# The output projection of a fused attention and multiplicative FFN kernel, taken apart a second time: 49 small matrix products for 64, with streamed weight sums

## The chip, the core and the metric

The kernel runs on one NeuronCore of a Trainium2 chip. Its engines work side by side, each with an instruction queue of its own: TensorE (PE in the profile, with PEld for its weight loads), VectorE (DVE), ScalarE (ACT), GpSimd (POOL) and SyncE (SP), which here only issues DMAs. Time is the device time of one execution in microseconds (us), lower is better. A run of the kernel is compared by the median of several executions; one further execution is profiled, and every duration below comes from that one.

## What is computed

The attention is linear (no softmax): for each of 8 batches and 8 heads, with 576 tokens of 64 features, `kv = k^T v`, `out = q kv`, then an RMS norm over the 64 features with a gain. The result is laid out as 4608 tokens by 512 features and goes through

```
def _moe_ref(x, w1, w2, w3, w_out):
    a = x @ w1                 # 512 -> 1024
    b = x @ w2
    h = a * b @ w3             # 1024 -> 1024
    return (h @ w_out)         # 1024 -> 512, float32
```

All matrix products are done in float32. The weights arrive as 8-byte floats, and the kernel turns them into float32 itself.

## The kernel before, in words

**Fold.** `w3 @ w_out` is computed first, once: a 1024 by 512 matrix, `w3o_sb`, in 2 halves of 8 chunks. For each chunk, ACT and DVE convert raw words to float32 (`conversion`, L130), PE turns the chunk of w3 (`turn_w3`, L464), ACT copies it, and PE multiplies it with the chunk of w_out (`fold_chunk`, L477). Chunk numbers below count from 0, so the second chunk is chunk 1 (the "chunk 2" of the change's name). In this stage the order of DVE, ACT, SP and PE is written out by hand. `keep_warm` (L253) issues products of a constant matrix, whose results nobody reads.

**Groups.** The tokens are then worked on in 9 groups of 512: first 512 tokens of batches 0 to 6 (T = 0 to 6), then the 64 left-over tokens of all 8 batches together (T = 8), then batch 7 (T = 7). For each group:

- *Gates* (L613): four passes p = 0 to 3, each a two by two block product in 7 block products where plain multiplication has 8 (`winograd`, L489; the scheme is Winograd's form of Strassen's). It needs sums of blocks on both sides: `sum_w` and `combine_x`. Each pass has 28 matrix products of 128x128 by 128x256, and leaves `a * b` for 256 of the 1024 features in `ab`.
- *Projection* (L632): `ab @ w3o`, once more by 7 block products, of 8 matrix products each. Its sums are `sum_ab(p)` over `ab` (4 DVE operations per p) and `combine_w3o` over the weights (once, in group 0).

A matrix product in float32 is two instructions (MATMUL) in the trace, each with its own LDWEIGHTS. So 28 products are 56 MATMUL rows, and a whole projection of 56 products is 112.

The attention of the next batch is cut into 8 pieces (`steps`), which `between()` puts between the block products of the gates. `combine_x` for the next group is written ahead of the projection. PE's order is the written order; DVE, ACT and GpSimd run in an order that a scheduler fixed at build time, each engine strictly in its order. SP's DMA queue is in order too: a DMA whose wait is not over holds all behind it.

**Memory in the projection.** `allocate_projection` (L569) reuses the four conversion buffers (`raw`) for the sums over `ab`, the sums over `w3o` and the two output tiles. Results leave PSUM through `keep` (an ACT copy) and `done` (a DVE addition). There are 5 PSUM banks for all of this.

Lines L482 to L535 of the kernel before, which the prediction names by the profile's groups: L496 is the one line of all block products, L509 the ACT copy, L548 and L549 the DVE sums over `ab` and `w`, L538 the DVE sums over `x` and `w3o`, L618 and L619 the copy and the product of the last gate block (c21), L622 and L623 the same for the others.

Of the kernel before, what the change touches and what calls it, by code (L numbers as in the profile page):

```python
# [11 lines left out]
FP32 = mybir.dt.float32  # L12
# [8 lines left out]
def kernel(  # L21
# [32 lines left out]
    nc = tc.nc  # L54
# [58 lines left out]

    NF = KF // 2

    ab = [const.tile([P, 4, N], FP32, name=f"ab{p}") for p in range(NF)]

    w_sb = const.tile([P, KF, 2, NP, P], FP32, name="w_sb")
    w3o_sb = const.tile([P, KF, DM], FP32, name="w3o_sb")
# [10 lines left out]
    def conversion(n, dst, raw, cols=slice(0, 1024)):  # L130

        dst, raw = (t if len(t.shape) == 3 else t[:, cols] for t in (dst, raw))
        if raw.dtype == FP32:
            yield
            nc.vector.tensor_copy(out=dst, in_=raw)
            return
        words = raw.bitcast(U32).rearrange("p (n w) -> p n w", w=2)
        lo, hi = words[:, :, 0], words[:, :, 1]

        low = ab[NF - 2 + n % 2].rearrange("p i t -> p (i t)")[:, cols]  # L140
        low_bits = low.bitcast(U32)
        if len(dst.shape) == 3:
            wide = dict(c=dst.shape[1])
            lo, hi, low, low_bits = (
                t.rearrange("p (c n) -> p c n", **wide) for t in (lo, hi, low, low_bits)
            )
        dst_bits = dst.bitcast(U32)
        nc.scalar.activation(low, lo, AF.Copy, scale=2.0 ** -51, bias=2.0)  # L148
        nc.scalar.activation(dst, hi.bitcast(FP32), AF.Abs)
        yield  # L150
        nc.vector.scalar_tensor_tensor(  # L151
            out=low_bits, in0=hi, scalar=0x80000000, in1=low_bits,
            op0=ALU.bitwise_and, op1=ALU.bitwise_or,
        )
        nc.vector.tensor_scalar(
            out=dst, in0=dst, scalar1=LEAST, scalar2=MOST, op0=ALU.max, op1=ALU.min
        )
        nc.vector.tensor_scalar(
            out=dst_bits, in0=dst_bits, scalar1=3, scalar2=None, op0=ALU.logical_shift_left
        )  # L160
        nc.vector.tensor_tensor(out=dst_bits, in0=dst_bits, in1=low_bits, op=ALU.add)  # L161
# [12 lines left out]
    def raw_tile():  # L174
        return conv_pool.tile([P, 1024], w1.dtype, name="raw", bufs=RAW)
# [32 lines left out]
    def conversions(n):  # L208

        what, i = todo[n]  # L210
        if what == "w":
            return [conversion(n, w_sb[:, i].rearrange("p w c f -> p (w c f)"), raws[n])]
        if what == "b":
            return [conversion(n, chunks[:, 2 * i:2 * i + 2, 0, :], raws[n])]
        dst = chunks[:, i].rearrange("p w f -> p (w f)")
        cuts = [0, 1024] if i else [0, 256, 512, 1024]
        return [conversion(n, dst, raws[n], slice(a, b)) for a, b in zip(cuts, cuts[1:])]

    begun = []
# [40 lines left out]
    def attention(b):  # L260
# [74 lines left out]
        def product(h):  # L335

            o_ps = [bank(ps_at, "at") for _ in range(2)]
            for m in range(4):  # L340
                r, e = 2 * h + m // 2, m % 2
                for i in range(2):
                    n = 2 * m + i
                    for t in range(2):
                        tokens = slice(t * L, (t + 1) * L)
                        for l in range(2):
                            rows = slice(l * D, (l + 1) * D)
                            nc.tensor.matmul(  # L348
                                o_ps[l][tokens, n * D:(n + 1) * D],
                                lhsT=qT[r][rows, e, i, tokens],  # L350
                                rhs=kv_b[rows, e, r, :],
                                start=True,
                                stop=True,
                            )
            xn = st[h] = work.tile([P, 2, 2, 4, D], FP32, name="xn")
            return norm(o_ps, [xn[:, :, l].rearrange("p i m d -> p m i d") for l in range(2)])

        def product_left():
# [105 lines left out]
    def turn_w3(half, c):  # L464
        t_ps = bank(ps_at, "at").rearrange("p (m f) -> p m f", m=NH)
        for m in range(NH):
            src = chunks[:, c, 0, m * P:(m + 1) * P]
            nc.tensor.transpose(t_ps[:, m, :], src, ident)  # L468

        w3T[half, c] = ab[c % 4 // 2][:, c % 2 * 2:c % 2 * 2 + 2, :].rearrange(  # L470
            "p i (a f) -> p (i a) f", f=P
        )
        nc.scalar.copy(w3T[half, c], t_ps)
# [3 lines left out]
    def fold_chunk(half, c, ms):  # L477
        if c == 0 and 0 in ms:
            sums_ps[half] = [bank(ps_mm, "mm") for m in range(NH)]
        for m in ms:  # L480
# [4 lines left out]
            if c == KF - 1:  # L485
                nc.scalar.copy(w3o_sb[:, half * NH + m, :], sums_ps[half][m])


    def winograd(lhsT, rhs, chunks, done, between=lambda: None):  # L489

# [14 lines left out]
            return ps  # L505

        def keep(name, ps):
            t = late_pool.tile([P, 2, N], FP32, name=name[0] if name[0] == "u" else name)
            nc.scalar.copy(t, ps)  # L509
            return t  # L510

# [40 lines left out]
    def run(*step_lists):  # L552

        for steps in zip(*step_lists):
            for step in steps:
                step()
# [1 line left out]
    xb, wa, aa, ob = {}, {}, {}, {}  # L558
    xc = const.tile([P, 3, NP // 2, N], FP32, name="xc")
    free = {("w", 0): const.tile([P, 3, 2, NP // 2, P], FP32, name="ws0")}  # L560
    o_sbs = []

    def allocate():

# [3 lines left out]

    def allocate_projection():  # L569

        blocks = []
        for i in range(RAW):
            words = raw_tile().bitcast(FP32).rearrange("p (n t) -> p n t", t=N)
            if i + 1 < RAW:
                blocks += [words[:, n] for n in range(8)]
            else:
                o_sbs.extend(
                    words[:, 4 * n:4 * n + 4].rearrange("p (m j) t -> p m (j t)", m=2)
                    for n in range(2)
                )  # L580
        for p in range(NF):
            free["ab", p], free["w3o", p] = blocks[6 * p:6 * p + 3], blocks[6 * p + 3:6 * p + 6]

    def parts(t):
        return [t[:, i] for i in range(3)]
# [1 line left out]
    def combine_x(T):  # L587
        xb[T] = {f"b{i + 1}{j + 1}": xT[T][:, i, j] for i in range(2) for j in range(2)}
        return combine(xb[T], parts(xc))
# [7 lines left out]
        return sums(wa[p], parts(free["w", p]))  # L597

    def sum_ab(p):
        aa[p] = {name: ab[p][:, i, :] for i, name in enumerate(("a11", "a21", "a12", "a22"))}  # L600
        return sums(aa[p], free["ab", p])

    def combine_w3o(p):
# [4 lines left out]
        return combine(ob[p], free["w3o", p])  # L608


    AB_OF = {"c11": 0, "c12": 1, "c21": 2, "c22": 3}

    def gates(T, p, between):  # L613
        def done(name, one, two):
            dst = ab[p][:, AB_OF[name], :]
            if two is None:
                c = late_pool.tile([P, N], FP32, name="c21")
                nc.scalar.copy(c, one[:, 0, :])  # L618
                nc.vector.tensor_mul(dst, c, one[:, 1, :])  # L619
                return  # L620
            c = late_pool.tile([P, 2, N], FP32, name="c")
            nc.vector.tensor_add(c, one, two)  # L622
            nc.vector.tensor_mul(dst, c[:, 0, :], c[:, 1, :])  # L623

        winograd(
            lambda name, w, c: wa[p][name][:, w, c, :],
            lambda name, c: xb[T][name][:, c, :],
            NP // 2, done, between,
        )


    def project(T, between=lambda: None, last=False):  # L632
        def store(half):
            if T < B:
                rows = out[T * S:T * S + G, :].rearrange("(p j) f -> p j f", j=J)
# [6 lines left out]
                        out=out[b * S + G:(b + 1) * S, :], in_=o_sbs[half][l * L:(l + 1) * L, m, :]  # L642
                    )

        def done(name, one, two):
            half, j = int(name[1]) - 1, int(name[2]) - 1
            dst = o_sbs[half][:, :, j * N:(j + 1) * N]
            if last:

                rows = out[T * S:T * S + G, j * N:(j + 1) * N].rearrange("(p j) f -> p j f", j=J)  # L650
                parts = ((0, 1), (1, 2)) if two is None else ((0, 2),)
                for a, b in parts:
                    if two is None:
                        nc.scalar.copy(dst[:, a:b], one[:, a:b])
                    else:
                        nc.vector.tensor_add(dst, one, two)
                    queue = nc.scalar if a else nc.sync
                    queue.dma_start(out=rows[:, 2 * half + a:2 * half + b, :], in_=dst[:, a:b])
                return
            if two is None:  # L660
                nc.scalar.copy(dst, one)
            else:
                nc.vector.tensor_add(dst, one, two)  # L663
            if name in ("c11", "c21"):
                store(half)

        winograd(
            lambda name, m, p: aa[p][name][:, m * P:(m + 1) * P],
            lambda name, p: ob[p][name],
            NF, done, between,  # L670
        )


    ctx.enter_context(tc.manual_schedule(engines={mybir.EngineType.PE}))
# [4 lines left out]
    with tc.manual_schedule(  # L679
# [22 lines left out]
        for c in range(KF):  # L702
# [13 lines left out]
            fold_chunk(0, c, range(NH - 1))  # L716
            turn_w3(*((0, c + 1) if c + 1 < KF else (1, 0)))
            fold_chunk(0, c, [NH - 1])


        first = batch(0)
# [41 lines left out]
    for n, T in enumerate(groups):  # L763
# [19 lines left out]
        last = n + 1 == NG  # L783
        if T and not last:
            run(combine_x(groups[n + 1]))
        project(T, between if T == 0 else lambda: None, last)
        if T == 0:
            run(combine_x(1))


# [28 lines left out]
```

## Time and profile before

| What | us |
|---|---|
| median of 5 executions (lowest, highest) | 812.66 (811.55, 813.68) |
| the profiled execution's own time | 813.68 |
| its span, from the first to the last instruction | 811.9 |
| PE busy in it | 802.2 (99%) |
| DVE, ACT, POOL busy | 364.6, 264.8, 1.8 |
| projection of T = 1, first product to the next group's first product | 228.88 to 253.06 |
| data moved by DMA | 59.53 MB, mean 73 GB/s |

An engine's idle time matters only where PE waits for it. The granted TensorE clock was 0.998 of full speed over the span, so a stretch of PE rows shows how many instructions there were and little else, apart from the first 20 us. Times of rows are counted from the span's start.

### The profile page before, as it was taken

How to read it: one execution, taken by the hardware profiler on the slowest of the kernel's cores; microseconds unless marked ns; L12 is line 12 of the kernel's file. 1: busy time of each engine (PE TensorE's matmuls, PEld its weight loads, DVE VectorE, ACT ScalarE, POOL GpSimd, SP SyncE). 2: the span in 40 equal slices, each digit the busy share in tenths (PEclk: the TensorE clock that was granted, in tenths of full speed). 3: DMA queues.
4: the chain of work that ended last, by engine and by line, in shares of the span. 5: the costliest groups of instructions: out<-in, count | busy, mean ns of one | idle time of the engine just before them, and what ended most of it. 6: DMA issues, size and time to landing. Idle time of an engine off the chain costs nothing.

```text
span 811.9 us, 12622 instructions
## 1 busy us (share of the span) xinstructions
PE 802.2 (99%) x5335; PEld 677.8 (83%) x5335; DVE 364.6 (45%) x680; ACT 264.8 (33%) x501; POOL 1.8 (0%) x8
## 2 busy tenths in 40 slices
PE   7999999999999999999999999999999999999998
PEld 4455788888888888888888888888888888888887
DVE  6967997325431544154315441553145415422431
ACT  5677643233312432133214331332133212211220
POOL 0000000000000000000000000000000000000000
PEclk9999999999999999999999999999999999999999
DMA  9996551123102410231023101410100010002001
GB/s 314 300 328 182 185 144 40 53 78 92 52 1 79 104 53 1 78 92 53 0 78 105 52 1 54 116 53 1 55 24 1 1 52 1 1 0 52 1 0 52
DMA packets 60811, 59.53 MB, mean 73 GB/s; under 512 B 15316, under 2 KB 57300, under 8 KB 60756
## 3 DMA queue, kind: packets, MB, share of 16 engines
q1 hardware_dynamic: 60608, 58.60, 23.4%
q8 instruction: 42, 0.69, 0.4%
q10 hardware_dynamic: 148, 0.13, 0.0%
q14 instruction: 13, 0.11, 0.0%
HBM read 49.28 MB, written 9.44 MB: 72 GB/s over the span
## 4 chain that ended last, share of the span: by engine, by line
PE 98%; DMA 1%; DVE 0%; SPq 0%; ACT 0%; issue 0%; ACTq 0%
PE mm L496 81%; PE mm L481 7%; PE at L278 3%; PE at L348 2%; PE at L297 2%; PE at L381 2%; DMA raw<-in_moe_w_out_dram 1%; PE at L468 1%; PE at L366 0%; SPq L184 0%; PE at L390 0%; PE at L307 0%; DVE chunks L161 0%; DVE ab L151 0%; ACT ab L148 0%
## 5 line engine op out<-in xcount | busy, mean ns | idle before, releaser
L496 PE MATMUL mm<-xT,w_sb 128*128 128x256 f32 x768 | 176.2, 379 | 0.0
L496 PEld LDWEIGHTS mm<-xT,w_sb 128*128 128x128 f32 x768 | 145.9, 190 | 20.3 <-issue 0.5
L496 PE MATMUL mm<-xc,ws 128*128 128x256 f32 x576 | 130.3, 379 | 0.0
L509 ACT COPY u<-mm 128x512 f32<-128x512 f32 x90 | 52.7, 585 | 218.4 <-PE mm L496 215.1
L496 PEld LDWEIGHTS mm<-xc,ws 128*128 128x128 f32 x576 | 109.4, 190 | 15.0 <-ACT p L509 0.2
L622 DVE TENSOR_TENSOR c<-mm,u 128x512 f32<-128x512 f32 x36 | 24.8, 690 | 189.4 <-PE mm L496 189.4
L509 ACT COPY p<-mm 128x512 f32<-128x512 f32 x90 | 52.7, 585 | 134.6 <-PE mm L496 134.6
L496 PE MATMUL mm<-w3o_sb,ab 128*128 128x256 f32 x432 | 96.2, 379 | 0.0
L496 PEld LDWEIGHTS mm<-w3o_sb,ab 128*128 128x128 f32 x432 | 82.1, 190 | 11.2
L496 PE MATMUL mm<-xc,w_sb 128*128 128x256 f32 x288 | 69.5, 384 | 0.0
L496 PE MATMUL mm<-raw 128*128 128x256 f32 x288 | 63.6, 379 | 0.0
L481 PE MATMUL mm<-chunks,ab 128*128 128x512 f32 x128 | 61.5, 613 | 1.1 <-DVE chunks L161 1.1
L496 PEld LDWEIGHTS mm<-raw 128*128 128x128 f32 x288 | 54.7, 190 | 7.4
L496 PE MATMUL mm<-xT,ws 128*128 128x256 f32 x256 | 60.9, 381 | 0.0
L496 PEld LDWEIGHTS mm<-xc,w_sb 128*128 128x128 f32 x288 | 52.5, 190 | 7.0
L496 PEld LDWEIGHTS mm<-xT,ws 128*128 128x128 f32 x256 | 47.2, 190 | 6.2 <-ACT p L509 0.3
L623 DVE TENSOR_TENSOR ab<-c 128x256 f32<-128x256 f32 x108 | 45.8, 424 | 3.4
L663 DVE TENSOR_TENSOR raw<-mm,u 128x512 f32<-128x512 f32 x8 | 5.5, 692 | 82.9 <-issue 46.2
L481 PEld LDWEIGHTS mm<-chunks,ab 128*128 128x128 f32 x128 | 22.6, 195 | 23.4 <-issue 17.9
L622 DVE TENSOR_TENSOR c<-p,u 128x512 f32<-128x512 f32 x36 | 24.9, 691 | 35.4 <-ACT u L509 35.4
L317 DVE TENSOR_REDUCE inv<-sq 128x8 f32<-128x512 f32 (+1 forms) x40 | 23.5, 628 | 32.3 <-ACT sq L316 32.3
L496 PE MATMUL mm<-w3o_sb,raw 128*128 128x256 f32 x144 | 32.7, 380 | 0.0
(90 smaller groups left out, 768.3 us busy)
## 6 DMA issues: line engine op xcount, KB each, us to landing
raw<-in_moe_w_dram SPq DMA_DIRECT2D x31, 512.0 KB, 7.4
k_sb<-in_k_dram SPq DMA_DIRECT2D x32, 256.0 KB, 4.6
v_sb<-in_v_dram SPq DMA_DIRECT2D x32, 256.0 KB, 4.5
q_sb<-in_q_dram SPq DMA_DIRECT2D x32, 256.0 KB, 3.2
out_dram<-raw SPq DMA_DIRECT2D x14, 512.0 KB, 2.6
raw<-in_moe_w_out_dram SPq DMA_DIRECT2D x7, 512.0 KB, 8.1
out_dram<-raw SPq DMA_DIRECT2D x9, 128.0 KB, 2.4
kl_sb<-in_k_dram SPq DMA_DIRECT2D x8, 128.0 KB, 5.6
```

The lines of the kernel that those rows point to most:

```text
L278: nc.tensor.matmul(kv_ps[e * D:(e + 1) * D, r - rs[0], :], lhsT=k_sb[:, e, cols] if j < J else kl[:, 2 * r + e, :], rhs=v_sb[:, e, cols] i ...
L297: nc.tensor.transpose(qt_ps[:, e, i, :], q_sb[:, e, i * P:(i + 1) * P], ident)
L317: nc.vector.tensor_reduce(out=inv[:, i], in_=sq.rearrange("p (h d) -> p h d", d=D), axis=AX.X, op=ALU.add)
L348: nc.tensor.matmul(o_ps[l][tokens, n * D:(n + 1) * D], lhsT=qT[r][rows, e, i, tokens], rhs=kv_b[rows, e, r, :], start=True, stop=True,)
L381: nc.tensor.transpose(t_ps[:, j, :], st[r // 2][:, j // 2, j % 2, m:m + 2, :], ident)
L468: nc.tensor.transpose(t_ps[:, m, :], src, ident)
L481: nc.tensor.matmul(sums_ps[half][m], lhsT=w3T[half, c][:, m, :], rhs=chunks[:, c, 1, :], start=(c == 0), stop=(c == KF - 1),)
L496: nc.tensor.matmul(ps[:, u, :], lhsT=lhsT(a_name, u, c), rhs=rhs(b_name, c),  start=(u == 0 and c == 0 and to is None), stop=(c == chunks ...
L509: nc.scalar.copy(t, ps)
L622: nc.vector.tensor_add(c, one, two)
L623: nc.vector.tensor_mul(dst, c[:, 0, :], c[:, 1, :])
L663: nc.vector.tensor_add(dst, one, two)
```

## The change

1. **A second level.** In groups 1 to 8 in the order of work (all but T = 0) each of the 7 block products of the projection is itself done by 7 smaller ones. A block product was 8 products of 128x128 by 128x256; it becomes 14 of 128x128 by 128x128. Both levels need sums on both sides.
2. **Sums over `ab`, inner level** (`sum_inner`): 4 operations of 128 partitions by 256 for each of the 7 blocks and each group. Blocks 0, 1 and 3 go to DVE, blocks 2, 4, 5 and 6 to GpSimd. `sum_inner(n + 1)` is written ahead of `products(n)`; the results go into two sets of buffers in turn.
3. **Sums over the weights, inner level** (`prepare_b`): made once on GpSimd after group 0's projection, 28 operations, and written to memory: 7 parts of 128 x 1792 floats, 917 KB each. Each projection reads all 7 parts again (`load_b`), into three buffers that are used in turn. SP issues all of these DMAs.
4. **Leaving PSUM.** A block now leaves as 7 small blocks of 128x128 (ACT copies of 512 and 384 columns, or DVE additions of that size), and `finish` puts them together in 4 DVE operations per output quarter.
5. **Layout.** `ab` becomes two tiles in place of four; `xn` has one buffer in place of two; the last group's output leaves in four DMAs of 256 KB from SP.
6. **Fold.** Chunk 1 is converted in two pieces of 512 in place of one of 1024, and four products of `keep_warm` follow chunk 0's last product.

Its core:

```diff
-        cuts = [0, 1024] if i else [0, 256, 512, 1024]
+        cuts = [[0, 256, 512, 1024], [0, 512, 1024], [0, 1024]][min(i, 2)]
...
             fold_chunk(0, c, [NH - 1])
+            if c == 0:
+                keep_warm(4)
...
+    def prepare_b():
+        for n, y in enumerate(b_blocks()):
+            b11, b12, b21, b22 = (
+                y[:, 2 * i:2 * i + 2, j * P:(j + 1) * P] for i in range(2) for j in range(2)
+            )
+            stage = late_pool.tile([P, 3, 2, P], FP32, name="stage")
+            t1, t2, t4 = (stage[:, i] for i in range(3))
+            nc.gpsimd.tensor_sub(t1, b12, b11)
+            nc.gpsimd.tensor_sub(t2, b22, t1)
+            nc.gpsimd.tensor_sub(b12, b22, b12)
+            nc.gpsimd.tensor_sub(t4, b21, t2)
+            nc.sync.dma_start(
+                out=w3o_l2[n, :, 0:1024].rearrange("p (f n) -> p f n", n=N), in_=y
+            )
+            nc.sync.dma_start(
+                out=w3o_l2[n, :, 1024:PART], in_=stage.rearrange("p i c n -> p (i c n)")
+            )
+    def load_b():
+        n = len(loaded_b)
+        t = streams[n % len(streams)]
+        nc.sync.dma_start(out=t, in_=w3o_l2[n % 7])
+        loaded_b.append(t)
+    def sum_inner(n):
+        s1, s2, s4 = ab_sums
+        x = [ab[0][:, :, 0], s1, s2, s4, ab[0][:, :, 1], ab[1][:, :, 0], ab[1][:, :, 1]][n]
+        a11, a12, a21, a22 = (
+            x[:, 2 * j:2 * j + 2, i * P:(i + 1) * P] for i in range(2) for j in range(2)
+        )
+        s1, s2, s4 = inner_sums[n % 2]
+        engine = nc.vector if n in (0, 1, 3) else nc.gpsimd
+        engine.tensor_add(s1, a21, a22)
+        engine.tensor_sub(s2, s1, a11)
+        engine.tensor_sub(s4, a12, s2)
+        engine.tensor_sub(a21, a11, a21)
+        inner[n] = [a11, a12, a22, s1, s2, s4, a21]
+    def project_twice(T, last):
...
+        def products(n, ps=None):
+            new = ps is None or n == 5
+            if ps is None:
+                ps = [bank(ps_mm, "mm").rearrange("p (i n) -> p i n", n=P) for _ in range(2)]
+            a11, a12, a22, s1, s2, s4, s3 = inner[n]
+            w = loaded_b[7 * done[T] + n]
...
+            for place, x, y in (
+                (0, a11, b11), (3, a12, b21), (1, a22, t4), (2, s1, t1), (6, s2, t2), (5, s4, b22),
+                (4, s3, t3),
+            ):
+                to, i = ps[place // 4], place % 4
+                for c in range(2):
+                    nc.tensor.matmul(
+                        to[:, i, :], lhsT=x[:, c, :], rhs=y[:, c, :],
+                        start=new and place // 4 not in seen,
+                        stop=(c == 1),
+                        skip_group_check=True,
+                    )
+                    seen.add(place // 4)
+            return ps
+        def keep(name, ps):
+            t = late_tile(name)
+            nc.scalar.copy(t[:, 0:4], ps[0])
+            nc.scalar.copy(t[:, 4:7], ps[1][:, 0:3])
+            return t
+        def finish(z, half, j):
...
+            nc.vector.tensor_add(z[:, 6], z[:, 6], z[:, 0])
+            nc.vector.tensor_add(z[:, 4:6], z[:, 4:6], wide(6))
+            nc.vector.tensor_add(dst[:, 1], z[:, 1:3], wide(4))
+            nc.vector.tensor_add(dst[:, 0], z[:, 3:6:2], z[:, 0:3:2])
...
+        def step(n, ps=None):
+            if n + 1 < 7:
+                sum_inner(n + 1)
+            ps = products(n, ps)
+            if len(loaded_b) < 7 * (NG - 1):
+                load_b()
+            return ps
+        sum_inner(0)
+        r1 = step(0)
+        p1 = keep("p1", r1)
+        r2 = step(1)
+        p5 = keep("p5", r2)
+        step(2, r1)
+        z = keep("u2", r1)
+        step(3, r2)
+        add(z, r2)
+        finish(z, 0, 1)
+        step(4, r1)
+        z = keep("u3", r1)
+        nc.vector.tensor_add(p5, p5, z)
+        finish(p5, 1, 1)
+        step(5, r2)
+        add(p1, r2)
+        finish(p1, 0, 0)
+        step(6, r1)
+        finish(keep("u4", r1), 1, 0)
...
         if T and not last:
             run(combine_x(groups[n + 1]))
-        project(T, between if T == 0 else lambda: None, last)
-        if T == 0:
-            run(combine_x(1))
+        if T:
+            project_twice(T, last)
+            continue
+        project(T, between)
+        run(combine_x(1))
+        prepare_b()
+        for _ in range(3):
+            load_b()
```

## The prediction, made before the changed kernel ran

> **What bounds the kernel now.** I read the page first: busy time, the slices, and the chain that ended last.
>
> ```profile
> span 811.9 us, 12622 instructions
> PE 802.2 (99%) x5335; PEld 677.8 (83%) x5335; DVE 364.6 (45%) x680; ACT 264.8 (33%) x501; POOL 1.8 (0%) x8
> ...
> PE   7999999999999999999999999999999999999998
> ...
> PE 98%; DMA 1%; DVE 0%; SPq 0%; ACT 0%; issue 0%; ACTq 0%
> ```
>
> PE is busy 99% and is 98% of the chain; in the slices it has room only at both ends. So a change gains what it takes out of PE's row, and loses whatever PE then waits for. Next I read PE's timeline around the projection of T = 1 (columns: start, length from first start to last end, then the group) and over the first 22 us:
>
> ```profile
> 7.47 1.28 PE L257 MATMUL mm<-ident 128*128 128x128 f32 x10
> 8.68 0.22 PE L700 MATMUL at<-ident,g_row 1*128 1x1 f32 x1
> 10.00 2.81 PE L481 MATMUL mm<-chunks,ab 128*128 128x512 f32 x6 [1.11 <-DVE chunks L161]
> 15.77 0.85 PE L468 MATMUL at<-ident,chunks 128*128 128x128 f32 x4 [2.95 <-DVE chunks L161]
> 16.41 5.14 PE L481 MATMUL mm<-chunks,ab 128*128 128x512 f32 x8
> 21.39 0.60 PE L468 MATMUL at<-ident,chunks 128*128 128x128 f32 x4
> ...
> 228.88 3.62 PE L496 MATMUL mm<-w3o_sb,ab 128*128 128x256 f32 x16
> ...
> 253.06 1.24 PE L496 MATMUL mm<-xT,w_sb 128*128 128x256 f32 x5
> ```
>
> The projection runs from 228.88 to 253.06: 24.18 us for 112 instructions, 216 ns each, without a gap. Nothing is waited for there today, because it starts with 16 instructions (3.46 us) on blocks that need no sum. DVE uses this cover:
>
> ```profile
> 226.90 0.68 DVE L622 TENSOR_TENSOR c<-mm,p 128x512 f32<-128x512 f32 x1
> 227.62 0.42 DVE L623 TENSOR_TENSOR ab<-c 128x256 f32<-128x256 f32 x1
> 228.08 0.42 DVE L549 TENSOR_TENSOR raw<-raw,ab 128x256 f32<-128x256 f32 x1
> 228.43 0.42 DVE L549 TENSOR_TENSOR ab<-ab 128x256 f32<-128x256 f32 x1
> 228.76 0.68 DVE L538 TENSOR_TENSOR xc<-xT,xc 128x512 f32<-128x512 f32 x1
> 229.36 0.68 DVE L538 TENSOR_TENSOR xT<-xT 128x512 f32<-128x512 f32 x1
> 229.97 0.41 DVE L619 TENSOR_TENSOR ab<-c,mm 128x256 f32<-128x256 f32 x1
> 230.30 0.68 DVE L538 TENSOR_TENSOR xc<-xT,xc 128x512 f32<-128x512 f32 x1
> 230.90 0.42 DVE L549 TENSOR_TENSOR raw<-ab,raw 128x256 f32<-128x256 f32 x1
> ```
>
> From start to start an operation of 256 columns takes 0.34 us and one of 512 takes 0.60. DVE works on until 231.3, which is 2.4 us into the projection.
>
> **Step 1, PE's own work.** A projection has 56 products of 256 columns now, 98 of 128 columns then, so 196 instructions. Their price is in the first fence: the same form, 128x128 by 128x128 in float32, ten in 1.28 us, and one lasts 0.275 (the group's median), so (1.28 - 0.275) / 9 = 111.7 ns from start to start. 196 x 0.1117 = 21.89 us, 2.29 less; 8 groups give **-18.3 us**. Lower bound of the price: the transposes of the same shape (8 in 1.04 us, one lasts 0.273) go at 109.6 ns, another -3.3 us in all. Upper bound: a wait at each block's start that is not hidden, some 0.1 us (the gap that the next step takes from a row) x 56 blocks = +5.6. I take the same form's row and no gap, since the rows of 256 columns keep 216 ns across their waits.
>
> **Step 2, the head of the projection.** The new block 0 needs inner sums over the first quarter of `ab`, and this quarter is complete only after the last pass of gates. Its three products without sums are 12 instructions, 1.34 us of cover in place of 3.46. In the changed program's order DVE reaches block 0's sums late: after the c11 addition come block 1's s1, the c11 product, block 1's s2, the outer s2 and s3, an xc, the c21 product, the xT, the outer s4, the last xc, and only then block 0's s1; then block 1's s4 and block 0's s2, s3 and s4. With the fence's steps, from 226.90: 227.50, 227.84, 228.18, 228.52, 228.86, 229.20, 229.80 (c21; 229.97 today, so its input is there or 0.2 late), 230.14, 230.74, 231.08, 231.68 for block 0's s1, and 233.04 for its s4, which ends at 233.46. PE is out of ready products at 230.22, and the last anchor is s4: a restart after DVE took 0.15 us at 10.00 (DVE's L161 ended at 9.85), so s4's and s3's products, 8 instructions, start at 233.61 and end at 234.50. Without a wait block 0 would end at 228.88 + 28 x 0.1117 = 232.01. The stall is 2.5 us. T = 3 and 5 have the same order. In T = 2 and 4 four more transposes (0.44) stand before the last gate product, so DVE is that much ahead: 2.1. T = 6 has one xc behind block 0's s1: 2.3. T = 8 has no attention pieces and two xc earlier: 2.2; T = 7 has no combine_x: 1.6. Sum 7.5 + 4.2 + 2.3 + 2.2 + 1.6 = **+17.8 us**. The waits are given back nowhere: PE's order is fixed.
>
> **Step 3, the rest of the projection: 0.** GpSimd's sums for block 2 may start when PE has used block 0's s1 (same buffers), four products before block 0's end, and are due in block 2's fourth product, some 6 us later. Blocks 4 to 6 follow in a row: block 4's may start 10.5 us after the gates' end (5.6 for block 0 with its stall, 3.13 for block 1, 1.8 into block 2) and the twelfth operation is due at 5.6 + 5 x 3.13 + 2.2 = 23.5. So GpSimd has 13.0 / 12 = 1.08 us for one operation. The trace has none of this form; its rows are a memset of 128x128 (0.20 us), one of 64x512 (0.52) and a select of 128x128 (0.29). Ends for 256 columns: 0.31 (between the memsets) and 1.2 (the select, doubled for the columns and again for the second input). I take 0.6, twice the select. ACT's copies (0.585 for 512, some 0.48 for 384 columns) and DVE's additions fit in a block of 3.13 us, each bank of PSUM being drained while the other pair fills.
>
> The streamed part is 917 KB, issued when block n ends and due two blocks later, 6.25 us. At the 382 GB/s of the stage from 10 to 20 us it takes 2.4 us, and a lone 256 KB load of q landed 2.8 us after its issue, 2.1 more than its own transfer. So 4.5 us, 1.7 to spare; it is late below some 245 GB/s, and the busiest slices of the page show 300 to 328. SP's issue (0.4 us) is in the spare. Bounds: 0 to 2 us per group.
>
> Group 0's preparation stands on GpSimd and SP beside group 0's projection. Behind its waiting DMAs on SP are loads of q, k and v, issued up to 14 us later than today (today k at 142 for a use at 183). The parts are read only from 228 on. 0, at most +5 once.
>
> **Step 4, fold: -2.6 us.** The gap of 2.95 us before 15.77 is PE waiting for chunk 1's conversion; then the clock drops, and the 8 instructions from 16.41 take 5.0 us where the next 8 take 3.5. In pieces, chunk 1's w3 half can be converted when it has landed (9.3) and turned at 12.7, right after chunk 0's three products. ACT does chunk 2's conversion (13.50 to 15.6) ahead of its copy for chunk 1, so the next products start at 16.25; with four products of keep_warm the longest gap is 1.4 us, and I take the clock to hold, as it did over the gap of 1.1. Chunk 2 is turned at 18.8 in place of 21.39. PE sets the pace from there. Bounds: -1.0 (clock drops all the same) to -2.8.
>
> **Step 5, the end: +1.5 us.** Today PE ends at 808.2, two ACT copies at 808.9. Then: the copy of 384 columns (0.5), four DVE operations of `finish` (1.6), and a last DMA of 256 KB as before.
>
> Sum: -18.3 + 17.8 - 2.6 + 1.5 = **-1.6 us** against this execution's own 813.68 (span 811.9 and 1.8 around it). That execution is 1.0 over the median of 812.66; from the median, **811.0**.
>
> **A rule that speaks against it.** The trace has no GpSimd operation beside a DVE one; DVE's 0.42 us holds beside a busy ACT, and by that row I add nothing. The Trainium skill, "SBUF — State Buffer" (Who interferes with whom), says that a DVE operation with two SBUF inputs and a GpSimd operation that reads SBUF exclude each other for a whole instruction. No row here shows it; by the rule, block 2's first sum could get in ahead of block 0's s4.
>
> **Rivals.** (a) *DVE and GpSimd hold each other up at the head.* GpSimd is released some 0.1 us before block 0's s4 starts; one operation of 0.6 in front of it costs 8 x 0.6 = 4.8: 815.8. For it: the two meet within 0.1 us; against: DVE may be first. (b) *Slower: GpSimd sets the pace.* Place: blocks 4 to 6; it decides from 1.08 us an operation; price 12 x (t - 1.08) per group. At 1.3 us that is 2.6 x 8 = 21: 832. Against: it needs more than my upper row. (c) *The stream is late:* below 245 GB/s, 1 us at each of two loads, 16 in all: 827. Against: DMA is 5% busy in this stage today. (d) *The clock drops in the new gap of 1.9 us,* as after 2.95: half speed for 3.4 us, 8 x 1.7 = 14: 825. (e) *The fold edit does nothing,* since ACT's order holds chunk 1's copy back: 811.0 + 2.6 = 813.6.
>
> **Numbers.** Forecast 0.55, over 806 to 813.5 for its own bounds (price 109.6; head 0.2 less per group); (e) 0.05; (a) 0.20, 813 to 818; (b) 0.08, (c) 0.07, (d) 0.05. The range leaves out the last three: 806 to 818. This kernel's measurement can tell 0.2%, 1.6 us. Of the forecast's 0.55, 0.42 lie under 811.03 and 0.13 within; (e) within; of (a) 0.05 within, 0.15 over. Faster 0.42, same 0.23, slower 0.35.
>
> **What would show it.** The rows of 128 columns at 111.7 ns; PE's waits for DVE's sums at block 0, some 2 us per group, the last for s4; GpSimd's row under 1.08 us and no PE wait for it or a DMA; the clock at full from 6 us on. I am wrong if PE waits inside blocks 1 to 6, or not at block 0.

## The result, and the profile after

The changed kernel takes **813.98 us** (median of 22 runs, 811.55 to 816.48), the kernel before 812.47 (42 runs): a ratio of 1.0016, with a 95% interval of 1.0009 to 1.0023, or +1.3 us (the two medians differ by 1.5) where -1.6 was forecast. The range held it, the direction did not. Its profiled execution took 813.48, its span is 811.7.

The page after, busy time and the chain that ended last:

```profile
PE 790.4 (97%) x6015; PEld 686.2 (85%) x6015; DVE 469.2 (58%) x924; ACT 283.4 (35%) x542; POOL 132.4 (16%) x164
...
PE 88%; DVE 8%; ACT 1%; DMA 1%; issue 1%; SPq 0%; DVEq 0%; ACTq 0%
```

PE has 11.8 us less to do, yet the span is no shorter, and DVE has come into the chain, where before PE held 98%. The place is the head of each second-level projection. PE's timeline there, for T = 1 (columns: start, length, group, in brackets PE's idle time before it and what ended it):

```profile
225.24 1.50 PE L751 MATMUL mm<-w3o_sb,ab 128*128 128x128 f32 x12
228.47 2.05 PE L751 MATMUL mm<-w3o_sb,raw 128*128 128x128 f32 x12 [1.73 <-DVE raw L710]
...
249.56 0.81 PE L499 MATMUL mm<-xT,w_sb 128*128 128x256 f32 x3
```

Twelve instructions that need no sum start at 225.24, and the next one only at 228.47. L710 is the addition that makes s1. DVE's timeline says why it is late:

```profile
225.53 0.68 DVE L541 TENSOR_TENSOR xc<-xT,xc 128x512 f32<-128x512 f32 x1
...
226.46 0.68 DVE L541 TENSOR_TENSOR xT<-xT 128x512 f32<-128x512 f32 x1
227.06 0.41 DVE L552 TENSOR_TENSOR raw<-ab,raw 128x256 f32<-128x256 f32 x1
227.40 0.68 DVE L541 TENSOR_TENSOR xc<-xT,xc 128x512 f32<-128x512 f32 x1
228.00 0.41 DVE L710 TENSOR_TENSOR raw<-ab 128x256 f32<-128x256 f32 x1
```

Three additions for the next group (L541), which starts 24 us later, stand in DVE's order ahead of the sum that PE waits for. The order is fixed at build time, so DVE cannot step past them.

The second thing to see is what such a wait does to the clock. These are the windows around T = 3's head (columns: window, its length, busy time and instructions of PE, PEld, DVE, ACT and POOL, granted clock, DMA share, GB/s):

```profile
391.00:393.00 2.00, 0.45 (x4) 0.45 (x4) 2.00 (x6) 0.00 (x0) 0.00 (x0) 1.00 0.00 0
393.00:395.00 2.00, 2.00 (x13) 1.70 (x12) 1.18 (x4) 0.58 (x1) 1.57 (x2) 0.82 0.04 8
395.00:397.00 2.00, 2.00 (x12) 2.00 (x11) 0.00 (x0) 0.48 (x1) 1.92 (x3) 0.50 0.18 32
```

PE issues nothing for most of the first window; 1.7 us after it has begun again, its granted clock falls to half, and its instructions stand 213 ns apart instead of 112. The windows make it some 3.4 us, and it costs 1.63 (this projection took 25.96 us, T = 1's 24.33). In this execution it came at T = 3 alone, although T = 1 and T = 5 have the same gap of 2.0 us.

PE's waits in the whole span (total, times, longest; only time after the modelled end of the instruction before counts, so these are smaller than the distances above):

```profile
PE mm L751 <- DVE raw L710: 10.1, 7, 1.7
...
PE mm L751 <- DVE raw L711: 1.8, 1, 1.8
...
PE mm L751 <- DMA w3o_sb<-w3o_l: 0.6, 1, 0.6
```

GpSimd is in the list only at the program's start (2.0 us for the constant matrix, as before the change). A streamed load is, once: in T = 6 it landed 6.7 us after its issue, where most took 4.4 to 5.1, and held PE up by 0.9 (two distances of 0.91 and 0.18 in place of 0.11).

**The balance of the two traces.** From the first product of T = 1's projection to the end, before takes 811.9 - 228.88 = 583.0 us, after 811.7 - 225.24 = 586.5. The 3.4 more are 1.6 of half clock, 0.9 of the late load, and 0.9 of everything that comes in every execution. What stands before T = 1 is 3.6 shorter.

### The profile page after: what moved, and what is told of

Same layout as the page of the kernel before. It is cut to its first block, busy times and chain, and to the rows that moved or that the text cites. A ratio compares the mean times of both kernels' runs of the same rounds, so it can differ in the third digit from the quotient of the medians.

```text
span 811.7 us, 14734 instructions
## 1 busy us (share of the span) xinstructions
PE 790.4 (97%) x6015; PEld 686.2 (85%) x6015; DVE 469.2 (58%) x924; ACT 283.4 (35%) x542; POOL 132.4 (16%) x164
## 4 chain that ended last, share of the span: by engine, by line
PE 88%; DVE 8%; ACT 1%; DMA 1%; issue 1%; SPq 0%; DVEq 0%; ACTq 0%
PE mm L499 54%; PE mm L751 19%; PE mm L481 7%; PE at L278 3%; PE at L348 2%; PE at L297 2%; DVE c L633 1%; PE at L381 1%; DVE xc L541 1%; DMA w3o_sb<-w3o_l 1%; DVE ab L634 1%; PE at L468 1%; DVE raw L552 1%; ACT u L512 1%; DMA raw<-in_moe_w_out_dram 1%
## 5 line engine op out<-in xcount | busy, mean ns | idle before, releaser
L512 ACT COPY u<-mm 128x512 f32<-128x512 f32 x74 | 43.3, 585 | 145.2 <-PE mm L499 141.8
L710 POOL TENSOR_TENSOR raw<-raw 128x256 f32<-128x256 f32 x8 | 11.7, 1458 | 500.6 <-PE mm L751 435.2
L751 PE MATMUL mm<-w3o_sb,raw 128*128 128x128 f32 x584 | 76.8, 281 | 8.3 <-DVE raw L710 8.3
L751 PEld LDWEIGHTS mm<-w3o_sb,raw 128*128 128x128 f32 x584 | 70.8, 194 | 11.3 <-DVE raw L710 9.5
L512 ACT COPY p<-mm 128x512 f32<-128x512 f32 x74 | 43.3, 585 | 87.6 <-PE mm L499 87.6
L751 PE MATMUL mm<-w3o_sb,ab 128*128 128x128 f32 x352 | 45.7, 275 | 0.6 <-DMA w3o_sb<-w3o_l 0.6
L762 ACT COPY u<-mm 128x512 f32<-128x512 f32 x24 | 14.1, 586 | 88.9 <-DVE raw L775 51.7
L751 PEld LDWEIGHTS mm<-w3o_sb,ab 128*128 128x128 f32 x352 | 42.9, 192 | 1.1 <-issue 0.8
```

The lines of the kernel that those rows point to most:

```text
L710: engine.tensor_add(s1, a21, a22)
L751: nc.tensor.matmul(to[:, i, :], lhsT=x[:, c, :], rhs=y[:, c, :], start=new and place // 4 not in seen, stop=(c == 1), skip_group_check=True,)
L762: nc.scalar.copy(t[:, 0:4], ps[0])
```

## The experiments

Each is an edit of the changed kernel unless it says otherwise. The kernel before ran beside them: 813.16 beside e1 to e4, 812.12 beside e5 to e8, 812.15 beside e9 to e12. The ratios are to these.

| Kernel | median us (runs) | ratio to before, 95% |
|---|---|---|
| e1 sums first, combine_x later | 796.85 (4) | 0.9807, 0.9791 to 0.9822 |
| e2 filler in the gap | 813.56 (11) | 1.0015, 1.0005 to 1.0026 |
| e3 no fold edit | 816.69 (6) | 1.0060, 1.0037 to 1.0083 |
| e4 before + fold edit | 810.94 (11) | 0.9977, 0.9968 to 0.9987 |
| e5 short loads | 813.67 (11) | 1.0021, 1.0007 to 1.0034 |
| e6 filler and short loads | 812.52 (11) | 1.0004, 0.9995 to 1.0013 |
| e7 sums first, short loads | 796.14 (4) | 0.9796, 0.9783 to 0.9810 |
| e8 before + two pieces | 810.62 (11) | 0.9980, 0.9971 to 0.9989 |
| e9 combine_x later | 799.13 (5) | 0.9840, 0.9826 to 0.9853 |
| e10 sums first | 795.46 (4) | 0.9799, 0.9780 to 0.9817 |
| e11 as e1, shorter end | 795.02 (4) | 0.9790, 0.9777 to 0.9804 |
| e12 as e1, again | 796.23 (4) | 0.9804, 0.9787 to 0.9821 |

### Is it DVE's order? e1, e9, e10, e12

e1 and e12 (the same kernel) make both moves, e10 the first and e9 the second alone:

```diff
             else:
+                if p + 1 == NF:
+                    sum_inner(0)
                 run(sum_ab(p))
...
-        if T and not last:
-            run(combine_x(groups[n + 1]))
         if T:
-            project_twice(T, last)
+            project_twice(T, last, lambda: run(combine_x(groups[n + 1])) if not last else None)
...
-        sum_inner(0)
         r1 = step(0)
+        then()
```

> Block 0's sums are written ahead of the last pass's outer sums, and combine_x behind block 0's products; nothing is left out. In DVE's new order block 0's s1 starts right behind the c11 product and its s4 right behind c21. My theory (the head's wait for DVE is the loss, and the clock's drop comes out of that wait): the eight head stalls of the changed kernel's trace, 2.45 + 2.05 + 2.45 + 2.05 + 2.45 + 2.3 + 2.1 + 1.7 = 17.55 us, all go, no instruction of a projection comes at 213 ns any more, and the granted clock is 0.999 or 1.0 in every run: 813.98 - 17.55 - about 1.8 for drops = 794.6. Rival, DVE and GpSimd hold each other up: GpSimd's first sums now start beside DVE's xc additions, which last 0.68 each; if GpSimd is held back by all of them, its twelve sums of blocks 4 to 6 come late and PE waits there: 797 to 800. Rival, the stream is late when blocks follow each other without the pause: PE waits for loads in blocks 2 to 5, 0.8 us at each: 800 or more. If the head stall was not the loss, the time stays over 810.

> The kernel with sums first and combine_x later once more, beside the three above, since its time of 796.85 rests on 4 runs. Expected 796.5 to 797.2, a clock of 0.999 or 1.0 in every run, and projections of 21.9 us. If the half clock still comes by chance after shorter gaps elsewhere, some runs lie 1.6 higher.

PE's timeline for T = 1 in e12, and DVE's:

```profile
225.64 1.50 PE L751 MATMUL mm<-w3o_sb,ab 128*128 128x128 f32 x12
226.98 1.50 PE L751 MATMUL mm<-w3o_sb,raw 128*128 128x128 f32 x12
```

```profile
225.26 0.42 DVE L710 TENSOR_TENSOR raw<-ab 128x256 f32<-128x256 f32 x1
...
226.93 0.42 DVE L712 TENSOR_TENSOR raw<-ab,raw 128x256 f32<-128x256 f32 x1
...
228.61 0.69 DVE L541 TENSOR_TENSOR xc<-xT,xc 128x512 f32<-128x512 f32 x1
```

s1 now starts before PE's first product, the additions for the next group come last, and the bracket at PE's second row is gone. A projection takes 21.88 us in place of 24.33. In T = 8 and T = 7 0.2 us stay, the wait for s4. So the head stall was the loss, and without it the granted clock was 0.999 or 1.0 in all 8 runs. The times are 1.6 to 2.3 us over the 794.6 that I expected. This difference isn't settled. Late loads may be a part of it: PE waited 0.5 us for one in e12's profile, and 1.0 in that of e7, the same kernel with loads that are short only behind T = 1 (796.14). The start of T = 1's projection differed by 2 us between profiles (225.24 in after, the earliest, to 227.37), and each median rests on 4 runs.

> Only combine_x is moved behind block 0's products; block 0's sums stay behind the outer sums. By DVE's new order and the changed kernel's rows for T = 1 (c11 product at 224.19, steps of 0.34 and 0.33): block 0's s1 at 225.53, c21 at 226.20, s2 at 226.53, s4 at 227.20 to 227.62, s3 to 227.95; PE wants s4 at 227.47 and can go on 0.15 after it. My theory (three xc and xT additions of 0.60 in front of the sums made most of the wait): a stall of 0.3 in T = 1, 3 and 5 and 0 to 0.2 in the others, 1.5 in all, no drop of the clock, 796.85 + 1.5 = 798.3. Rival, the wait came from the outer sums and c21, which stay in front: 805 or more.

> Only block 0's sums are written ahead of the last pass's outer sums; combine_x stays ahead of the projection. DVE's new order puts block 0's s1, s2, s3, c21, s4, then two outer sums, the three additions of combine_x, then block 1's s4 and s3: by the steps of the changed kernel's rows block 1's s4 ends at 229.75 and is wanted at 230.6. My theory (it is the place in DVE's order alone that counts, and what is pushed back is wanted later): no stall, no drop, 796.85 as with both. Rival, what is pushed back becomes late, block 1's sums in place of block 0's: 0.3 to 1 us per group, 799 to 804.

Either move is nearly enough. With combine_x later alone 0.3 us stay at T = 1, 3 and 5 as expected, but I had missed that T = 8 (which has two of its three additions earlier) and T = 7 (which has no combine_x) gain little from it: 1.5 us stay at each. These are the two waits that e9's list still has (it counts less than the whole delay, as said above):

```profile
PE mm L751 <- DVE raw L710: 1.6, 2, 0.8
```

With sums first alone (e10) the list has no wait for DVE in the projections: what is pushed back was wanted later still.

### Where the clock falls: e2

```diff
             for place, x, y in (
...
             ):
                 to, i = ps[place // 4], place % 4
+                if n == 0 and place == 2:
+                    keep_warm(6)
```

> Six products of the constant matrix (12 instructions, 1.34 us) stand ahead of the first product that needs a sum of block 0, in each of the eight second-level projections; nothing is left out. They only fill PE's wait, so the head stall stays. My theory (half clock for some 3.4 us after the long gap, in some groups of some runs): the gap shrinks from 2.0 to 0.6 us, the clock stays at full, the median falls by what the drops cost, about 1.1 drops of 1.65 us, plus 0.4 for group 7, where the wait is shorter than the filler: 812.5, and the runs lie within 2 us instead of 5. Rival, the spread has another cause (late loads, DMA): the median is 814.0 to 814.5 and the runs still spread over 4 to 5 us.

PE's timeline of e2 for T = 1:

```profile
228.66 1.50 PE L257 MATMUL mm<-ident 128*128 128x128 f32 x12
230.56 2.05 PE L753 MATMUL mm<-w3o_sb,raw 128*128 128x128 f32 x12 [0.40 <-DVE raw L710]
```

The stall is as long as before, but the idle bracket shrinks from 1.73 to 0.40. The mean clock of an execution also counts the time behind PE's last product: in e2's profile the clock is full up to 809 us and half for the last 2.7, and this alone gives 0.998 (e11's profile has 0.998 for the same reason). A stretch of 3.4 us at half clock takes off 0.002. So I count 0.998 or more as an execution without a drop: 10 of 11 runs of e2, against 7 of 23 executions of the changed kernel. In those 23, time follows the clock: 812.4 on average at 0.999 or 1.0 (6 of them), 814.4 below. All 23 together average 1.4 more than the six, which is a little less than one stretch at half clock (1.63) in each. So the drops are shown to come from the gap. But the median fell by 0.4, not by the 1.5 I expected. Where the clock was 0.999 or 1.0, e2 averages 813.8 (8 runs), 1.3 over the changed kernel's six; in its profile a load was late by 0.45 us, and T = 1's projection began at 227.3, 2.1 later than in after. What e2's runs lose there stays open.

### What late loads cost: e5, e6, e7

```diff
-        nc.sync.dma_start(out=t, in_=w3o_l2[n % 7])
+        m = PART if n < 7 else N
+        nc.sync.dma_start(out=t[:, 0:m], in_=w3o_l2[n % 7, :, 0:m])
```

> The changed kernel, but from the second projection on each streamed load fetches only the first 256 of a part's 1792 columns (128 KB for 896 KB), so the products use old values in the rest: the reload of the weight sums is left out in six sevenths. Everything else waits as before. My theory now: besides the clock's drops (about 1.3 in a run at 1.6 us) some loads land 6.7 us after issue in place of 4.5 and hold PE for 0.4 to 0.9 us each; the profiles showed 0.8, 0.45 and 1.6 us of this in one execution. So the median falls by about 1 us, to 813.0, and every gap of PE behind block 1 goes. Rival, the stream costs nothing that counts and the difference comes from elsewhere: 814.0. Rival, late loads are the main loss: 811.5.

> Both edits: six filler products in the head's gap and the short loads (six sevenths of each reload left out). My theory (what the changed kernel has lost against my sum are drops of the clock in the gap and late loads, and nothing else): 810.94 of the fold edit alone, plus the second level without either, -0.7 for the eight projections and +1.75 for the end, = 812.0. Rival, something else grows by chance, which neither edit touches, GpSimd or the start of the program: 813 or more, as with the filler alone (813.56).

> Block 0's sums first and combine_x behind the products, with the short loads (six sevenths of each reload left out). With sums first the median was 796.85, and 794.6 was expected. My theory (late loads make the rest): 795.3 to 795.8. Rival, the rest is the start of the program, whose loads land by chance up to 1 us later than in the profile of the changed kernel: 796.5 to 797.

The traces are plain, the times are not. In executions with full-size loads PE lost 0.9 us to late loads (after), 1.7 (e3), 0.45 (e2), 0.1 (e1), 1.0 (e10), 0.6 (e11), 0.5 (e12) and nothing (e9), on average 0.6. With short loads there were no such waits behind T = 1, whose own loads are whole (e7 waited 1.0 there). e6 is 1.0 us under e2, e7 0.7 under e1 but 0.1 under e12, the same kernel as e1; e5 is only 0.3 under the changed kernel, with a clock of 0.997 or less in 8 of 11 runs. Each difference is about as large as its interval. Late loads cost some 0.6 us by the traces, and the times neither confirm nor exclude it. With both the filler and the short loads, the ratio to before falls from 1.0016 to 1.0004: by this test half clock and late loads together are about 1 us, within an uncertainty as large.

### The fold: e3, e4, e8

e3 takes the two edits of the fold out of the changed kernel, e4 puts them into the kernel before, e8 only the first of them:

```diff
-        cuts = [0, 1024] if i else [0, 256, 512, 1024]
+        cuts = [[0, 256, 512, 1024], [0, 512, 1024], [0, 1024]][min(i, 2)]
```

> The changed kernel without its two edits to the fold (chunk 1 converted in one piece, no filler products after chunk 0); nothing is left out. By the two traces chunk 2 was turned 3.68 us earlier with the edits, and the first projection started 3.64 us earlier, so this should cost 3.6: 817.6. Of this, 1.7 is half clock after the gap of 2.95 us, which may not come in every run: if it comes in half of them, 816.8. If the fold's gain is swallowed later, 814.

> The kernel before with the two edits to the fold alone; nothing is left out. My theory (the gain at the fold is kept to the end, since PE bounds everything behind it): 812.47 - 3.6 = 808.9, or 809.7 if the half clock after the old gap came in half of the runs only. My prediction had -2.6: 809.9. The rival that the fold edit does nothing: 812.5.

> The kernel before with chunk 1 in two pieces and no filler products; nothing is left out. Half clock after the fold's long gap came in 13 of 23 runs of the kernel before (medians 813.5 with it and 811.6 without), and in none of 11 with both edits (810.94). If the shorter gap alone prevents it, 811.0 and clocks of 0.999 or 1.0 in all runs. If the filler is what prevents it, the pieces give some 0.6 only: two clusters near 811.0 and 812.9, median 812.

The same windows of before and of e3, which both convert chunk 1 in one piece:

```profile
16.00:18.00 2.00, 2.00 (x6) 1.06 (x5) 1.97 (x3) 1.34 (x2) 0.00 (x0) 0.53 1.05 379
```

```profile
16.00:18.00 2.00, 2.00 (x6) 0.89 (x6) 1.93 (x3) 2.00 (x3) 0.00 (x0) 1.00 1.07 374
```

In e3 PE waited 1.85 us there and kept its clock; in before it had waited 2.95 and lost it. By runs, the clock was below 0.999 in 24 of 59 runs of before, and these are 1.7 us slower than the others (813.4 and 811.7 on average). In e4 it was so in none of 11, in e8 in one of 11, so I put it down to the fold. Then the profile of before showed a case that comes in 4 of 10 executions. In median the fold edit gives 0.23% (e4), 1.9 us, with an interval of 1.1 to 2.6; the pieces alone give as much (e8), so the filler isn't needed. e3, the same question asked of the changed kernel, gives more, 1.0060 against 1.0016, but its interval is over twice as wide and holds e4's value. The 3.6 us between the two profiles were half clock in the one and an early start in the other: in after PE waited 1.3 us between its first products and T = 1, in e4, with the same fold, 2.8, and e4's T = 1 began 1.4 later (226.60). What makes the start vary isn't traced.

### The end: e11

```diff
...
+        z = late_tile("u4")
+        nc.scalar.copy(z[:, 0:4], r1[0])
+        nc.vector.tensor_add(z[:, 6], r1[1][:, 2], z[:, 0])
+        six = z[:, 6:7].to_broadcast([P, 2, P])
+        nc.vector.tensor_add(z[:, 4:6], r1[1][:, 0:2], six)
+        finish(z, 1, 0, 2)
```

> Sums first and combine_x later, and for the very last block ACT copies only the first 512 columns; DVE's first two additions read the other 384 from PSUM. The chain after the last product loses ACT's copy of 0.48: the end from the last product's start shrinks from 5.9 to 5.4, 796.3. Rival, DVE's additions that read PSUM wait or last that much longer: 796.8.

No gain: the time from the last product's start to the end is 5.8 us in both. Rows from e12's last 8 us, of ACT and of DVE:

```profile
787.58 0.48 ACT L763 COPY u<-mm 128x384 f32<-128x384 f32 x1 [0.75 <-PE mm L751]
```

```profile
787.62 0.43 DVE L774 TENSOR_TENSOR raw<-p 128x256 f32<-128x256 f32 x1
...
788.30 0.28 DVE L772 TENSOR_TENSOR u<-u 128x128 f32<-128x128 f32 x1
```

While ACT copies, DVE is still busy with the quarter before (L774), and it reaches the last one without a pause. At the end DVE is the bound, not ACT. Its first two additions last 0.28 and 0.42 us in e11 too, where they read PSUM. Why e11's median is 1.2 under e12's isn't shown; the two profiled executions took 794.84 and 795.04.

## Why the forecast failed, step by step

- **Step 1 held.** Products of 128 columns are 111.6 ns apart (forecast 111.7), and a projection without waits is 21.88 us (21.89).
- **Step 2 held in every stall, and missed what a stall does.** The stalls are 2.45, 2.05, 2.45, 2.05, 2.45, 2.3, 2.1 and 1.5, 17.4 us in all (17.8; the 1.7 for T = 7 in e1's expectation counts the last product's own length), in the order of DVE's row as it was worked out; e1, e9 and e10 show the mechanism. What failed is the price of such a gap: the sum put half clock at nothing, and the sign "the clock at full from 6 us on" did not come. I had rival (d), half clock after all eight gaps, at 14 us and 0.05, or none. In truth it comes after some: after 4 of the 24 gaps in the profiles of after, e3 and e5 (gaps of 1.7 to 2.0 us), and after none of the three of 1.1 us in T = 7. Over the 23 executions it comes to +1.4 us.
- **Step 3: 0 was forecast; +0.6 by the traces.** GpSimd's operation takes 0.73 us (taken 0.6, limit 1.08), and PE never waited for it: rival (b) is excluded. Rival (c), two late loads in every group, did not come. Rival (a) is excluded too: block 0's s4 took 0.41 to 0.42 us in all eight groups, though GpSimd's first sum began 0.08 us ahead of it at T = 1. A typical load lands after 4.4 to 5 us as worked out (4.5), but now and then one takes 5.9 to 6.7, against a budget of 6.25; I had taken the typical one for all.
- **Step 4: -2.6 was forecast, -1.9 measured** (e4, 1.1 to 2.6). The step went by one execution, in which the clock had fallen. The runs show that it falls in 4 of 10, so the -2.6 could not be taken off the median as a whole. Rival (e) is excluded by e4's interval.
- **Step 5: +1.5 was forecast, +1.7 measured** (5.8 us from the last product's start to the end, 4.1 before). But the row that bounds it is DVE's, not ACT's copy.

Steps 1, 2 and 5 together were +1.0, and the traces give +0.9. The sum fails by what differs from execution to execution: half clock +1.4 and late loads +0.6, both put at nothing, and a gain at the fold that is 0.7 smaller. That is 2.7 us, and 2.9 were missed. One check from other runs: the changed kernel's six runs at 0.999 or 1.0 average 812.4 and e4's eleven 810.9, and the 1.5 between them are the 0.9 of the traces and the 0.6 of the loads. The sizes remain estimates all the same, since e6, which takes half clock and late loads away together, gained only 1.0, with an uncertainty as large.

## What to carry to other kernels

When an order is fixed at build time, look in it at what stands ahead of the one result that the bounding engine wants first: here one call that moves up (e10, 795.46 us) turns a change of +0.16% into one of -2.0%, with no work removed. A gap has two prices, its length and what the clock may lose after it, and the second comes in some executions only: read it from the clocks of many runs, not from the one that was profiled. The same goes for a gain that the profile seems to offer.

## What the hardware showed

**Half clock after gaps of 1.7 and 2.0 us.** The Trainium skill, "TensorE: Matmul & The Clock Gate" (HAM oscillation), sums its rule up as no idle gap over about 3.4 us. Here the clock halved after start-to-start gaps of 1.7 and 2.0 us, for about 3.4 us, in some executions and not in others. The same page ("The HAM clock gate") says that the activity window is free-running. The traces agree: in every profile the times between two changes of the granted clock are whole multiples of 3.413 us (114, 1 and 121 of them in after; 114, 1, 93, 1 and 27 in e3; 66, 1 and 169 in e5; 3, 1 and 232 in before), and the first change lies elsewhere each time (5.1, 7.3, 6.7 and 5.9 us). Cut along these stretches, after's T = 1 and T = 3 differ, though their gaps are equally long (the number behind the comma is PE's busy time, the third from the end the clock):

```profile
227.01:230.42 3.41, 1.95 (x13) 1.65 (x14) 3.08 (x9) 0.58 (x1) 1.16 (x1) 1.00 0.00 0
230.43:233.83 3.40, 3.40 (x33) 3.40 (x33) 1.00 (x3) 1.06 (x2) 2.38 (x4) 1.00 0.51 152
390.85:394.26 3.41, 1.71 (x11) 1.41 (x12) 3.33 (x9) 0.58 (x1) 0.91 (x1) 1.00 0.00 0
394.27:397.67 3.40, 3.40 (x19) 3.40 (x18) 0.00 (x0) 0.48 (x1) 2.63 (x4) 0.50 0.27 60
```

T = 3's gap lies whole in one stretch, T = 1's across two. Of the 24 gaps, the three that leave PE busy for 1.68 to 1.71 us of a stretch (T = 3 of after and e3, T = 1 of e5) were all followed by half clock; of the others, with 1.84 and more, one was (T = 8 of e3, 2.00). So what looks like chance is for the most part where the gap lies against these stretches. No exact limit comes out of these runs.

**GpSimd is held up by DVE, not the other way, at the head.** The first GpSimd sums of T = 1, in after and in e12:

```profile
229.26 1.41 POOL L710 TENSOR_TENSOR raw<-raw 128x256 f32<-128x256 f32 x1 [60.98 <-PE mm L751]
230.75 0.73 POOL L713 TENSOR_TENSOR raw<-raw 128x256 f32<-128x256 f32 x1
```

```profile
227.67 3.41 POOL L710 TENSOR_TENSOR raw<-raw 128x256 f32<-128x256 f32 x1 [58.98 <-PE mm L751]
```

A GpSimd operation of this form takes 0.73 when DVE is idle, but 1.41 and 3.41 here, and both times it ends 0.58 us after the last of DVE's operations in a row (230.09 and 230.50). DVE's row is not slowed meanwhile: its sums of 256 columns take 0.41 to 0.42 each. Later, when GpSimd has work in a row, DVE's sums of 0.42 take 0.61 to 0.94 in e12. The rule that the prediction weighed, that the two exclude each other (the Trainium skill, "SBUF — State Buffer", Who interferes with whom), agrees; what it cost was hidden, since neither of the two was late for PE.
